# Moving the first batches' weight products, banks and score work in a fused attention and leaky-ReLU kernel

## The chip, the cores and the metric

The kernel runs on one core of one Trainium2 chip. The metric is the device time of one execution in microseconds (us); lower is better. A core has five engines with queues of their own, each worked off in order: TensorE (PE; its weight loads are listed apart as PEld), VectorE (DVE), ScalarE (ACT), GpSimd (POOL) and SyncE (SP), which here issues transfers only. Matmul results go to PSUM, a memory of eight banks of 128 partitions x 512 fp32 values, from which DVE or ACT copies them to SBUF.

## What is computed

```python
B, H, S, Ns, D = 8, 8, 512, 32, 64          # x: (B,H,S,D), state: (B,H,Ns,D)
scores  = x @ state^T / sqrt(D);  a  = softmax(scores);  xread = a @ state     # S rows
scores2 = state @ x^T / sqrt(D);  a2 = softmax(scores2); sread = a2 @ x        # Ns rows
rows = concat([xread, sread], axis=2) -> (B*(S+Ns), H*D) = (4352, 512)
h = rows @ w_in                 # w_in: 512 x 2048
out = max(0.01*h, h) @ w_out    # w_out: 2048 x 512, fp32 result
```

## The kernel before, in words

Products are done in bf16 with fp32 sums. For each batch b the kernel does not form xread. It multiplies the state by w_in first: M = state @ w_in, block by block, 2 x 128 rows by 2048 columns, made in four **quarters** of 512 columns (`a_m`, line 356; copied from PSUM to SBUF by `m_evict`, line 376). Then the hidden layer of the batch is aT (the softmax weights, transposed) times M: sixteen column blocks j of 128, each two matmuls of 512 columns (`ff1`, line 386; for batch 0 `ff1_0`, line 927, two blocks at a time), each followed by the leaky ReLU on ACT (`Prelu`). The second product with w_out runs as `piece` (line 590: four matmuls of 512 columns for rows i and a quarter jq of the 16 blocks) for batch 0 and half of batch 1, and as Strassen-Winograd products of 256 columns for the rest. A **unit** (`Fast.unit`, line 657) is one step of those, two matmuls for batches 2 to 7; `Batch.run(n)` runs n of them. `Half` is the same for the second half of batch 1.

A matmul of a_m or a_scores uses 64 rows and 32 columns of the PE array; eight of these run side by side and are listed as 64*32. The spreads of the head use 128*32, all large products 128*128.

The order of the instructions on every engine is that of the program text (`manual_schedule`, line 52); only the waits come from the framework. PSUM is handed out by tags: "ph" and "py" are two banks each, used in turn, "sc" and "big" are a pair of neighbouring banks each. A new tile in a tag waits until the reader of the old one is done.

**Head** (lines 772 to 1017). Batch 0 has a special softmax in two halves u. For each half PE transposes x (`x0_half`), makes the scores twice (`scores0`, `rows0`), DVE finds the maximum (`max0`) and splits it in a high and a low bf16 part (`split0`: hi, lo), PE subtracts it from the scores by 32 small matmuls (`spread0`, line 816), ACT takes the exponential (`exp0`), PE sums it (`sum0`), DVE takes the reciprocal (`recip0`), PE spreads that (`recip0_rows`) and DVE multiplies (`probs0`, line 864, gives aT). Between the two spreads stand two matmuls on zeros (`spin(2, "py")`, line 900). Then come batch 0's products ff1_0, with the remaining quarters of M and batch 1's quarter 0 between them, batch 0's second scores (`a_scores`, `a_max2`), batch 1's casts, transposes, scores and quarters 1 to 3, with `piece` products between.

The head's loads are issued by POOL in the order w_in chunks 0 to 3 (one chunk holds the columns of one quarter), w_out chunk 0, batch 1's x in two halves, w_out chunks 1 and 2, batch 2's x, w_out chunk 3.

**Batches 2 to 7** (lines 1059 to 1192). Step s of sixteen runs ff1 block s of batch b, some units of the batch before or of the batch itself, as many as the list PACE (PACE2 for b = 2) says, and parts of the next batch's softmax. At s = 10 the first three quarters of the next batch's M are made, in "big", "sc" and "ph". In the last batch the blocks 4 to 11 are made by `FastLast` (line 500: 14 small products `pl`, whose partial sums DVE and ACT copy to tiles `ls`), two to a step; at s = 8 `a_sread` (line 311) makes the batch's sread: 16 matmuls into `psr`, in tag "big", copied by two ACT instructions into sr_t (line 322). At s = 13 `x_sums` reads sr_t, and after the loop `FastIn` multiplies it.

Of the kernel before, what the change touches and what calls it, by code (L numbers as in the profile page):

```python
# [9 lines left out]
P = 128  # L10
B, H, S, D = 8, 8, 512, 64
NS = 32
DFF = 2048
DM = 512
# [5 lines left out]
BF16 = mybir.dt.bfloat16  # L20
FP32 = mybir.dt.float32
# [6 lines left out]
def kernel(  # L28
# [15 lines left out]
    mpool = ctx.enter_context(tc.tile_pool(name="mpool", bufs=2))  # L44
# [84 lines left out]
    def spin(n, tag):  # L129
        p = psum.tile([P, S], FP32, name="pspin", tag=tag, bufs=2 if tag in ("ph", "py") else 1)  # L130
        for _ in range(n):
            nc.tensor.matmul(p[:], lhsT=idle[:, :P], rhs=idle[:], start=True, stop=True)  # L132

    stbd = consts.tile([P, NK, 2, NS], BF16, name="stbd")
    st1 = consts.tile([P, P], BF16, name="st1")
    groups = ((2, 4), (4, 8))
# [40 lines left out]


    class Attn:
        pass

    def a_open(a, b):
        a.b = b
# [165 lines left out]

    def a_m(a, c, tag):
        if c == 0:
            a.M = mpool.tile([P, 2, DFF], BF16, name="M", tag="M")
        if tag in ("ph", "py", "phpy"):
            pm = [psum.tile([P, DM], FP32, name="pm", tag=t) for t in (tag[:2], tag[-2:])]  # L360
            at = [t[:] for t in pm]
        else:
            pm = psum.tile([P, 2, DM], FP32, name="pm", tag=tag, bufs=1)
            at = [pm[:, g, :] for g in range(2)]
        for k in range(NK):
            for g in range(2):
                v, r = (k // 2, 2 * (k % 2) + (g ^ (k // 2))) if a.b == 0 else (g, k)
                nc.tensor.matmul(  # L368
                    at[v][NS * r:NS * (r + 1)],
                    lhsT=st_of(a, g, k),  # L370
                    rhs=w_in_bf[D * g:D * (g + 1), k, DM * c:DM * (c + 1)],
                    start=True, stop=True,
                )
        return pm
# [388 lines left out]

    OWN = 15
    PACE = (1, 4, 4, 4, 3, 4, 4, 3, 4, 4, 4, 4, 3, 4, 3, 3)
    PACE2 = (0,) * 10 + (3, 3, 2, 2, 2, 3)

    att_of = [Attn() for _ in range(B)]
    a0, a1, a2 = att_of[:3]
# [127 lines left out]
    rows0(1)  # L897
    spread0(scn[0], m[0], False)
    exp0(0)
    spin(2, "py")  # L900
    spread0(scn[1], split0(m[1]), False)
    exp0(1)
    sum0(0)
    q = [recip0(0)]
    pm = a_m(a0, 0, "sc")
    for g in range(2):
        SCA(a0.M[:, g, :DM], pm[:, g, :])
    sum0(1)
    q.append(recip0(1))
    for u in range(2):  # L910
        recip0_rows(u, q[u])
        probs0(u)
    m_evict(a0, 1, a_m(a0, 1, "big"), VEC)

    h0 = hpool.tile([P, 16, S], BF16, name="hT", tag="hT")

    def open_ff1_0(tag):  # L920
        if tag == "sc":
            pr = psum.tile([P, 2, S], FP32, name="php", tag=tag, bufs=1)
            return pr, [pr[:, 0], pr[:, 1]]
        ph = [psum.tile([P, S], FP32, name="ph", tag=tag) for _ in range(2)]
        return ph, [p[:] for p in ph]
# [22 lines left out]
    relu0(t0, 0)  # L948
    relu0(t2, 2)
    m_evict(a0, 2, a_m(a0, 2, "big"), VEC)  # L950
    m_evict(a1, 0, a_m(a1, 0, "ph"), VEC)
    for j, tag in ((4, "py"), (6, "sc"), (8, "py"), (10, "ph"), (12, "py"), (14, "ph")):
        t, bk = open_ff1_0(tag)
        for g in range(2):
            ff1_0(bk, j, g)
        relu0(t, j)
        if j == 8:
            m_evict(a0, 3, a_m(a0, 3, "big"), VEC)
            a_scores(a0)
            a_max2(a0)  # L960
    nc.vector.memset(stf[0][:, 0, D - 1:D + 1], 0.0)
# [6 lines left out]

    for g in range(2):
        a_exp2(a0, g)  # L970
    for i in (0, 1):
        piece(0, h0, i, 0)
    wide = psum.tile([P, 2, DM], FP32, name="pyw", tag="big", bufs=1)
    for u in range(2):
        ps = psum.tile([P, NT, 2, P], BF16, name="pxt2", tag="ph")
        for t in range(NT):
            for v in range(2):
                h = NK * u + 2 * v
                nc.tensor.transpose(
                    ps[:, t, v, :], a1.xb[:, t, h:h + 2, :].rearrange("p h d -> p (h d)"), ident[:]  # L980
                )
        VEC(a1.xT[:, :, 2 * u:2 * u + 2, :], ps[:])
        piece(0, h0, 2 + u, 0, bank=wide[:, u])
    a_scores(a1)
    m_evict(a1, 1, a_m(a1, 1, "ph"), SCA)
    a_shift(a1)
    a_max2(a1)
    for i in (0, 1):
# [71 lines left out]
    for b in range(2, B):  # L1060
# [20 lines left out]
        for s in range(16):  # L1081
            fast = nxt is None and 4 <= s < 12
            if fast:
                n = 1 if s in (7, 11) else 2
                k = PACE[s]
                for i in range(n):
                    fl.product()
                    units((i + 1) * k // n - i * k // n)
            elif s == 11:
                fill(s)  # L1090
            if not fast:
                ff1(a, hT, 4 + s if nxt is None and s < 4 else s)
            if s == 0:
                if b + 2 < B:
                    load_x(b + 2, nc.sync)
                a_a2t(a)
                if before:
                    for n in (0, 1):
                        before.f.sums(n, 4, 8)
            elif s == 1:  # L1100
                if nxt is not None:
                    a_scores(nxt)
                m_evict(a, 3, a_m(a, 3, "big"), SCA)
                if b == 2:
                    a_sread_rows([a0])
                elif b % 2:
                    a_sread_rows([att_of[b - 2], att_of[b - 1]])
                if b == 2:
                    half.f.sums(2)
                    a_shift(nxt, 0)  # L1110
                elif nxt is not None:
                    a_shift(nxt)
                if b + 2 < B:
                    open_xb(b + 2)
                    for h in range(0, H, 2):
                        cast_x(b + 2, h, h + 2, POO)
                if before:
                    before.f.sums(2, 4, 8)
            elif s == 3:
                if before:  # L1120
                    before.f.sums(3)
                if nxt is not None and b > 2:
                    a_max2(nxt)
            elif s == 4:
                if b == 2:
                    state_t(1)
                elif b == 4:
                    sread_t(0, 3)
                elif b == 7:
                    sread_t(1, 4)  # L1130
            elif s == 8:
                if nxt is None:
                    a_sread(a)
            elif s == 12:
                for n in range(3):
                    now.f.sums(n, 0, 4)
            if nxt is None:
                if s == 1:
                    fl = FastLast(a, hT)
                    fl.sums()  # L1140
                elif s in (6, 10):
                    fi.w_sum({6: 1, 10: 3}[s])
                elif s == 13:
                    fl.flush()
                    fi.x_sums()
            elif b >= B - 3 and s == 14:
                if b == B - 3:
                    fi = FastIn(None)
                fi.w_sum(2 * (b - (B - 3)))
            if s == (9 if b == 2 else 7) and b + 2 < B:  # L1150
                a_open(att_of[b + 2], b + 2)
                a_xt_dma(att_of[b + 2])
            if nxt is not None:
                if b == 2 and s < 11:
                    if s in (8, 9):
                        a_exp2(nxt, s - 8)
                elif s == 5:
                    a_exp(nxt)
                elif s in (7, 8):
                    a_exp2(nxt, s - 7)  # L1160
                    if s == 7:
                        a_probs(nxt)
                elif s == 11:
                    a_probs2(nxt)
                elif s in (12, 13):
                    SCA(nxt.M[:, s - 12, DM:2 * DM], pm1[:, s - 12, :])
            if std:
                i, jq = std.pop(0)
                piece(1, h1, i, jq)
            elif b == 2 and half.units:  # L1170
                half.run(7)
                if s == 4:
                    a_shift(nxt, 1)
                    half.f.sums(3)
                    weights_sum(3)
                    a_max2(nxt)
                elif s == 6:
                    a_exp(nxt)
                elif s == 8:
                    a_probs(nxt, 0)  # L1180
            elif s != 11 and not fast:
                fill(s)
            if s == 10 and nxt is not None:
                pm0 = a_m(nxt, 0, "big")
                pm1 = a_m(nxt, 1, "sc")
                pm2 = a_m(nxt, 2, "ph")
                for g, copy in enumerate((VEC, SCA)):
                    copy(nxt.M[:, g, 2 * DM:3 * DM], pm2[g][:])
                m_evict(nxt, 0, pm0, SCA)
                if b == 2:  # L1190
                    a_probs(nxt, 1)
# [91 lines left out]
```

## Time and profile before

| What | Value |
|---|---|
| median of 3 runs | 203.49 us (203.1 to 204.0) |
| the profiled execution | 203.36 us |
| its span, first to last instruction | 201.6 us |
| PE busy | 195.9 us, 2000 matmuls |
| DVE, ACT, POOL busy | 159.5, 145.0, 42.6 us |
| granted TensorE clock | 1.0 |
| head: first product of batch 0 | 13.56 us |
| head: first piece (py) | 22.20 us |
| w_in chunks landed | 9.00, 11.54, 15.36, 17.48 us |
| w_out chunks landed | 20.08, 25.27, 28.20, 33.75 us |
| batch 1's x, two halves landed | 21.61, 22.90 us |

The table's lower part is read from the trace, in us from the start of the span. In the lines of a timeline further down, the first number is the start, the second the time from the start of the first to the end of the last instruction of the group, then the engine, the line of the kernel, the operation, output<-inputs, rows*columns of the array, the shape and how many. In the lines of waits, the numbers are the total in us, how often, and the longest. An instruction's duration contains its latency, so durations of neighbours on one engine overlap; what an instruction costs its engine is the step to the next start.

### The profile page before, as it was taken

What the parts mean: (1) busy time and instruction counts of PE and PEld (TensorE: products, weight loads), DVE (VectorE), ACT (ScalarE), POOL (GpSimd) and SP (SyncE); (2) the same over time, 40 slices, a digit from 0 to 9 for tenths busy, and PEclk for the clock granted to TensorE, in tenths of its full rate; (3) what the DMA queues carried; (4) which work ended last, traced back from release to release, by engine and by line L of the source; (5) the groups of instructions that cost most, each with busy time, mean ns of one, the idle gap of its engine ahead of it and who ended that gap; (6) DMA issues with size and microseconds to landing.
All of it is one profiled execution on the core that took longest, in us unless ns stands there. A gap on an engine that the chain in (4) does not pass through costs nothing.

```text
span 201.6 us, 4848 instructions
## 1 busy us (share of the span) xinstructions
PE 195.9 (97%) x2000; PEld 129.2 (64%) x2000; DVE 159.5 (79%) x241; ACT 145.0 (72%) x267; POOL 42.6 (21%) x69
## 2 busy tenths in 40 slices
PE   7899999999999999999999999999999999999993
PEld 2543444444377567766776677676767688799882
DVE  1676679899989889985997599779978977995612
ACT  3459839589869886978697868787878768767710
POOL 8931002021009005200410040200020014104250
PEclk9999999999999999999999999999999999999999
DMA  6999995999794995549343945250029101310035
GB/s 198 218 206 277 232 301 99 133 311 238 131 210 127 123 282 96 104 167 274 81 78 124 281 75 99 107 156 5 0 86 173 31 3 66 142 55 3 0 90 170
DMA packets 39733, 27.99 MB, mean 139 GB/s; under 512 B 25312, under 2 KB 36704, under 8 KB 39712
## 3 DMA queue, kind: packets, MB, share of 16 engines
q1 hardware_dynamic: 34512, 20.88, 43.3%
q0 software_dynamic: 4912, 6.55, 15.9%
q10 hardware_dynamic: 288, 0.26, 0.6%
q8 instruction: 15, 0.25, 0.5%
q14 instruction: 6, 0.05, 0.1%
HBM read 17.30 MB, written 8.91 MB: 130 GB/s over the span
## 4 chain that ended last, share of the span: by engine, by line
PE 96%; DVE 1%; ACT 1%; issue 0%
PE yq L666 40%; PE ph L389 22%; PE py L596 7%; PE pm L368 4%; PE pyw L596 3%; PE pf L463 3%; PE yu L666 3%; PE pspin L132 3%; PE ph L929 2%; PE pl L552 2%; PE sc L207 1%; PE psn L333 1%; PE phw L400 1%; PE php L929 1%; DVE M L382 1%; ACT xT L791 1%
## 5 line engine op out<-in xcount | busy, mean ns | idle before, releaser
L394 ACT ACTIVATE hT<-ph 128x512 bf16<-128x512 f32 x100 | 58.9, 605 | 18.0 <-PE ph L389 17.6
L389 PE MATMUL ph<-aT,M 128*128 128x512 bf16 x200 | 57.8, 379 | 0.0
L666 PEld LDWEIGHTS <-su 128*128 128x128 bf16 x448 | 42.9, 98 | 13.8 <-DVE su L655 0.8
L666 PEld LDWEIGHTS <-hT 128*128 128x128 bf16 x312 | 30.1, 98 | 13.5 <-issue 2.0
L666 PE MATMUL yq<-tw_xf,su 128*128 128x256 bf16 x208 | 29.6, 273 | 0.0
L666 PE MATMUL yq<-w_out_bf,hT 128*128 128x256 bf16 x208 | 29.2, 273 | 0.0
L105 POOL CAST xb<-xl 128x512 bf16<-128x512 f32 (+1 forms) x21 | 14.1, 709 | 59.0 <-DMA xl<-in_x_dram 44.6
L389 PEld LDWEIGHTS <-M 128*128 128x128 bf16 x200 | 19.4, 98 | 7.3 <-issue 0.8
L655 DVE TENSOR_TENSOR su<-hT 128x1024 bf16<-128x1024 bf16 x26 | 18.1, 698 | 7.1 <-ACT hT L394 7.1
L675 ACT COPY sv<-yq 128x512 f32<-128x512 f32 (+1 forms) x28 | 15.4, 555 | 2.1 <-PE yq L666 1.4
L736 POOL TENSOR_TENSOR yo<-sv,sv 128x512 f32<-128x512 f32 x6 | 7.8, 1302 | 40.3 <-ACT sv L675 23.3
L596 PE MATMUL py<-w_out_bf,hT 128*128 128x512 bf16 x64 | 16.0, 379 | 0.0
L596 PEld LDWEIGHTS <-hT 128*128 128x128 bf16 x96 | 9.0, 98 | 10.8 <-issue 0.9
L666 PE MATMUL yq<-tw_x,su 128*128 128x256 bf16 x104 | 14.6, 273 | 0.0
L666 PE MATMUL yq<-w_out_bf,su 128*128 128x256 bf16 x104 | 14.5, 272 | 0.0
L382 ACT CAST M<-pm 128x1024 bf16<-128x1024 f32 x13 | 13.2, 1014 | 0.9 <-PE pm L368 0.9
L666 PE MATMUL yq<-tw_x,hT 128*128 128x256 bf16 x96 | 13.6, 273 | 0.0
L678 DVE TENSOR_TENSOR yo<-yq,sv 128x512 f32<-128x512 f32 x17 | 11.6, 684 | 1.5 <-PE yq L666 1.5
L287 ACT ACTIVATE e<-sc,mcols 128x512 bf16<-128x512 f32 x16 | 11.1, 697 | 0.2 <-DVE mcols L281 0.2
L279 DVE TENSOR_REDUCE mcol<-sc 128x2 f32<-128x1024 f32 x8 | 9.7, 1214 | 0.0
L655 DVE TENSOR_TENSOR su<-su,hT 128x1024 bf16<-128x1024 bf16 x13 | 9.0, 692 | 0.4
L217 DVE TRANSPOSE_TENSOR_REDUCE mrow<-sc 128x32 f32<-128x1024 f32 x7 | 8.7, 1244 | 0.6 <-PE sc L207 0.5
(167 smaller groups left out, 295.7 us busy)
## 6 DMA issues: line engine op xcount, KB each, us to landing
xl<-in_x_dram SPq DMA_DIRECT2D x5, 1024.0 KB, 6.6
out_dram<-yo SPq DMA_DIRECT2D x10, 512.0 KB, 2.7
w_in_bf<-in_moe_w_in_dram POOLq DMA_DIRECT2D x4, 512.0 KB, 9.2
w_out_bf<-in_moe_w_out_dram POOLq DMA_DIRECT2D x4, 512.0 KB, 17.0
out_dram<-ysb SPq DMA_DIRECT2D x8, 256.0 KB, 6.6
xf<-in_x_dram SPq DMA_DIRECT2D x2, 512.0 KB, 4.8
x<-in_x_dram POOLq DMA_DIRECT2D x2, 512.0 KB, 14.0
xl<-in_x_dram POOLq DMA_DIRECT2D x1, 1024.0 KB, 19.4
```

The costliest lines, as they stand in the source:

```text
L105: copy(xs[b][:, :, h0:h1].rearrange("p t h d -> p h t d"), xl[b][:, h0:h1].rearrange("p h (t d) -> p h t d", t=NT),)
L217: nc.vector.tensor_reduce(out=m1[:], in_=flat.rearrange("p (c j) -> p c j", j=NS), axis=AX.X, op=ALU.max, apply_transpose=True,)
L279: nc.vector.tensor_reduce(out=m2[:], in_=a.sc[:], axis=AX.X, op=ALU.max, negate=True)
L287: nc.scalar.activation(out=a.e2[:, g], in_=a.sc[:, g, :], func=AF.Exp, bias=a.m2s[:, g:g + 1], scale=SCALE, accum_out=a.r2[:, g:g + 1],)
L382: copy(a.M[:, :, cols], pm[:])
L389: nc.tensor.matmul(ph[:], lhsT=a.M[:, g, P * j:P * (j + 1)], rhs=a.aT[:, g, :], start=(g == 0), stop=(g == 1),)
L394: nc.scalar.activation(out=hT[:, j, :], in_=ph[:], func=AF.Prelu, alpha=0.01)
L596: nc.tensor.matmul(y.py, lhsT=hT[:, j, P * i:P * (i + 1)], rhs=w_out_bf[:, j, :], start=(j == 0), stop=(j == 15),)
L655: (eng or nc.vector).tensor_tensor(out=S[n][:, ms], in0=u[:, ms], in1=v[:, ms], op=op)
L666: nc.tensor.matmul(bank[:, i, :], lhsT=lhs[:, m, P * i:P * (i + 1)], rhs=rhs[:, m, :], start=(first and m == 0 and (i == 0 or of is not No ...
L675: copy(t[:], bank)
L678: nc.vector.tensor_tensor(out=dst, in0=bank, in1=self.sv[n][:], op=ALU.add)
```

## The change

- `a_m` makes the tile M where there is none yet, so that a quarter may be made out of order.
- The two spins go. In their place stands quarter 0 of batch 1's M (in "py"); DVE copies its first half right behind the second half's lo part, ACT copies its second half behind the two copies of batch 0's quarter 0.
- Quarter 1 of batch 0's M is made right behind quarter 0, and not after the softmax; its copy stays where it was.
- The tags "py", "sc", "py", "sc", "py", "ph", "py", "ph" for the eight double blocks of batch 0 become "py", "sc", "ph", "sc", "py", "ph", "py", "big".
- The copy of batch 0's last quarter is split in two halves of 256 columns. Batch 0's second scores and their maximum come after block pair 10 and not after 8.
- Of batch 1's transposes, each half comes after one piece; scores and quarter 1 come before the last piece of the first four and not after it.
- PACE2 gives 1, 4, 3, 3, 2, 2 units at s = 10 to 15, where it gave 3, 3, 2, 2, 2, 3.
- `a_sread` of the last batch moves from s = 8 to s = 11.

```diff
     class Attn:
-        pass
+        M = None
...
     def a_m(a, c, tag):
-        if c == 0:
+        if a.M is None:
             a.M = mpool.tile([P, 2, DFF], BF16, name="M", tag="M")
...
-    PACE2 = (0,) * 10 + (3, 3, 2, 2, 2, 3)
+    PACE2 = (0,) * 10 + (1, 4, 3, 3, 2, 2)
...
     exp0(0)
-    spin(2, "py")
+    a0.M = mpool.tile([P, 2, DFF], BF16, name="M", tag="M")
+    pm1 = a_m(a1, 0, "py")
     spread0(scn[1], split0(m[1]), False)
+    VEC(a1.M[:, 0, :DM], pm1[0][:])
     exp0(1)
     sum0(0)
     q = [recip0(0)]
-    pm = a_m(a0, 0, "sc")
+    pm = [a_m(a0, 0, "sc"), a_m(a0, 1, "big")]
     for g in range(2):
-        SCA(a0.M[:, g, :DM], pm[:, g, :])
+        SCA(a0.M[:, g, :DM], pm[0][:, g, :])
+    SCA(a1.M[:, 1, :DM], pm1[1][:])
     sum0(1)
...
-    m_evict(a0, 1, a_m(a0, 1, "big"), VEC)
+    m_evict(a0, 1, pm[1], VEC)
...
-        if tag == "sc":
+        if tag in ("sc", "big"):
...
     m_evict(a0, 2, a_m(a0, 2, "big"), VEC)
-    m_evict(a1, 0, a_m(a1, 0, "ph"), VEC)
-    for j, tag in ((4, "py"), (6, "sc"), (8, "py"), (10, "ph"), (12, "py"), (14, "ph")):
+    for j, tag in ((4, "ph"), (6, "sc"), (8, "py"), (10, "ph"), (12, "py"), (14, "big")):
         t, bk = open_ff1_0(tag)
         for g in range(2):
             ff1_0(bk, j, g)
         relu0(t, j)
         if j == 8:
-            m_evict(a0, 3, a_m(a0, 3, "big"), VEC)
+            m3 = a_m(a0, 3, "big")
+            for c in range(0, DM, 2 * P):
+                VEC(a0.M[:, :, 3 * DM + c:3 * DM + c + 2 * P], m3[:, :, c:c + 2 * P])
+        elif j == 10:
             a_scores(a0)
             a_max2(a0)
...
-    for i in (0, 1):
-        piece(0, h0, i, 0)
-    wide = psum.tile([P, 2, DM], FP32, name="pyw", tag="big", bufs=1)
     for u in range(2):
+        piece(0, h0, u, 0)
         ps = psum.tile([P, NT, 2, P], BF16, name="pxt2", tag="ph")
...
         VEC(a1.xT[:, :, 2 * u:2 * u + 2, :], ps[:])
-        piece(0, h0, 2 + u, 0, bank=wide[:, u])
+    wide = psum.tile([P, 2, DM], FP32, name="pyw", tag="big", bufs=1)
+    piece(0, h0, 2, 0, bank=wide[:, 0])
     a_scores(a1)
     m_evict(a1, 1, a_m(a1, 1, "ph"), SCA)
+    piece(0, h0, 3, 0, bank=wide[:, 1])
     a_shift(a1)
...
-            elif s == 8:
-                if nxt is None:
-                    a_sread(a)
...
                 elif s in (6, 10):
                     fi.w_sum({6: 1, 10: 3}[s])
+                elif s == 11:
+                    a_sread(a)
```

## The prediction

> **What bounds the kernel now.** I read the page's busy shares and its chain first, then TensorE's (PE's) timeline at the three places that the change touches, the waits of its weight loads (PEld) there, and the timelines of ScalarE (ACT) and VectorE (DVE) beside them.
>
> ```profile
> PE 195.9 (97%) x2000; PEld 129.2 (64%) x2000; DVE 159.5 (79%) x241; ACT 145.0 (72%) x267; POOL 42.6 (21%) x69
> PE 96%; DVE 1%; ACT 1%; issue 0%
> ```
>
> PE is busy for 195.9 of 201.6 us and is 96% of the chain, so a change gains only what it takes out of PE's own queue where PE waits for nothing else. In a timeline the step from one start to the next tells the cost: a 512-wide matmul takes 0.216 in a run (eight of py in 1.73). In the head:
>
> ```profile
> 10.21 0.60 PE L132 MATMUL pspin<-idle 128*128 128x512 bf16 x2
> 10.74 0.24 PE L820 MATMUL scn<-ident,hi 128*32 128x128 bf16 x4
> ...
> 13.22 0.41 PE L368 MATMUL pm<-w_in_bf,stbd 64*32 64x512 bf16 x8
> 13.56 0.61 PE L929 MATMUL ph<-aT,M 128*128 128x512 bf16 x2
> ...
> 15.40 0.41 PE L368 MATMUL pm<-w_in_bf,stbd 64*32 64x512 bf16 x8
> 15.63 0.40 PE L368 MATMUL pm<-w_in_bf,st 64*32 64x512 bf16 x8
> 15.96 1.04 PE L929 MATMUL ph<-aT,M 128*128 128x512 bf16 x4
> ...
> 18.69 0.41 PE L368 MATMUL pm<-w_in_bf,stbd 64*32 64x512 bf16 x8
> 18.97 0.41 PE L207 MATMUL sc<-xT,stbd 64*32 64x512 bf16 x8
> 19.32 3.04 PE L929 MATMUL ph<-aT,M 128*128 128x512 bf16 x12
> 22.20 1.89 PE L596 MATMUL py<-w_out_bf,hT 128*128 128x512 bf16 x8
> ```
> ```profile
> PEld L929 <- DVE M L382: 0.6, 1, 0.6
> PEld L368 <- DMA w_in_bf<-in_moe_w_in_dram: 0.4, 1, 0.4
> PEld L820 <- DVE lo L836: 0.4, 1, 0.4
> ```
>
> See three waits: the second half's spread (10.74) waits for VectorE's lo part; the quarter at 15.40 waits for the third chunk of w_in; and twelve matmuls from 19.32 take 2.88 where 2.59 would do, because M's last quarter is not copied yet.
>
> **Head, before 15.40: worth nothing.** The two spins stand in a wait: lo runs on DVE 10.49 to 10.67, and the spread starts 0.07 later with or without them. Batch 1's quarter 0 goes there: eight 64x32-tile matmuls, 0.22, plus the price of changing tile shape. That price is in the rows: four pyw from 25.68 to 26.64 take 0.96 where the four from 24.37 take 0.86 (0.10 to go in), and the pm at 26.86 takes 0.33 where the sc before it takes 0.22 (0.11 to come out). So it runs from about 10.10 to 10.53, with 0.14 of cover; without cover it costs up to 0.43. Its chunk landed at 9.00 by the trace. Its copies fit: DVE's 0.68 behind lo, before the 11.59 where DVE idled 0.93; ACT's 0.59 at 13.0, where ACT idled 1.59 until 14.63. Quarter 1 of batch 0 moves from 13.22 to behind quarter 0 (11.49): 16 matmuls in one visit end at about 12.01, and the instruction behind waits for the exponential (ACT 11.42 plus 0.60) until 12.07 anyway; its chunk landed at 11.54. What this frees at 13.22 is taken back at once: the first product needs the first aT (DVE, two in 1.30 from 12.79, the first done near 13.45), so 0.06 is gained, and the quarter at 15.40 still needs the chunk that landed at 15.36. Zero, taken from that row.
>
> **Head, 15.40 to 22.20: -0.35.** (a) The quarter at 15.63 is gone: a visit of two takes 0.56, of one 0.34 (13.22): -0.22. (b) VectorE loses batch 1's two copies (0.68 each) and copies M's last quarter in two halves. With the quarter's matmuls now at about 18.48, the halves are done near 19.6 and 20.25, and the products that read them start at 20.1 and 21.0: the 0.29 goes, and 0.04 at 17.70 with it. (c) Quarter and scores, one visit before (0.62 from 18.69 to 19.32), become two with a product between: 0.33 each and 0.10 to go in once more, +0.14. (d) PE then runs close to ACT: the product on sc waits for its bank until relu(t2), ACT 15.61 plus 1.03, so 16.68 instead of 16.61: +0.07. Laid out on one line: 15.40, 15.74, 16.68, 17.54, quarter 18.48, product 18.81, scores 19.78, products 20.11 and 20.98, end 21.84 against 22.20; (a) to (d) give -0.34. Other banks are free in time: py since 15.6, ph at 17.6, big when its last half is copied (20.25, needed 20.98).
>
> The Trainium skill's page "TensorEngine Tiling (Array Packing)", section Tiling Modes, says that changing the tiling mode drains the engine. It speaks against (c), gives no figure, and the 0.10 and 0.11 above agree; without the split, (c) would be zero and the head -0.5.
>
> **21.84 to 65: nothing.** Pieces, transposes and scores are the same instructions in another order (transposes next to pieces show no price: 0.45 for eight at 23.92 and 25.23). The second transposes, now at 24.0, need batch 1's second half, cast on DVE by 23.62 after landing at 22.90; cover 0.3 where there was 1.6. The scores, at 25.41, need xT, done at about 25.35 on DVE. The later w_out chunks landed at 25.27, 28.20 and 33.75, needed at 26.8, 31.2 and 34.6. SP's and POOL's queues keep their order; xT of batch 2 landed at 39.43, needed at 39.9. So -0.35 is carried on.
>
> **PACE2: +0.1.** Before, three units (six 256-wide matmuls, 0.65) stand on each side of batch 3's three quarters of M, and two waits for a ph bank cost 0.14 (67.12 to 67.92 for six) and 0.12 (ahead of the product at 69.34).
>
> ```profile
> 66.34 0.84 PE L368 MATMUL pm<-w_in_bf,st_t 64*32 64x512 bf16 x24
> 67.12 0.83 PE L666 MATMUL yq<-w_out_bf,hT 128*128 128x256 bf16 x6
> 67.92 1.02 PE L389 MATMUL ph<-aT,M 128*128 128x512 bf16 x4
> ...
> 66.06 0.61 ACT L394 ACTIVATE hT<-ph 128x512 bf16<-128x512 f32 x1
> ```
>
> The last row is ACT's. After, four matmuls fewer stand ahead, so the quarters start 0.44 earlier, at 65.91 on this clock; but the third needs the ph bank which ACT frees at 66.67, a row that moves only with ACT's own queue. It starts at 66.72 instead of 66.78, the product after the eight matmuls at 67.93 instead of 67.92 with one unit (0.22) still owed, and the second wait (0.12) is gone: +0.1. If ACT kept ahead, both waits would go: -0.26. Both ends are kept; I take +0.1, by the ACT row.
>
> **Rows read later: +0.36.** Here what is moved was itself the filling of a wait:
>
> ```profile
> 167.23 0.60 PE L666 MATMUL yq<-w_out_bf,su 128*128 128x256 bf16 x4
> 167.67 0.63 PE L315 MATMUL psr<-a2T,xb 128*128 128x64 bf16 x16
> 168.14 0.38 PE L552 MATMUL pl<-lx,lw 128*128 128x256 bf16 x2
> ...
> 167.38 0.60 ACT L565 COPY ls<-pl 128x512 f32<-128x512 f32 x1
> 168.40 0.53 ACT L322 CAST sr_t<-psr 64x128 bf16<-64x128 f32 x2
> ```
>
> The product at 168.14 overwrites the bank that ACT copies until 167.98. Without psr's 0.47 it starts at 168.03, not 167.67. The next (168.79) waits for DVE's join (168.02 plus 0.69) and keeps 168.77. Later two waits shrink, because ACT has no sr_t copies (0.53) ahead of the next ls: 0.14 at 169.58, of which DVE's copy for the product at 170.34 leaves 0.11. At the new place, after 171.97, PE has no wait that psr could fill: the next product starts without one at 172.08, and the timeline to the end is back to back. So 0.47 is added and 0.11 gained: +0.36. Bounds: +0.47 with nothing gained, +0.2 if the two waits (0.14 and 0.10) and a little more go.
>
> **Sum.** -0.35 + 0.1 + 0.36 = +0.1 on the profiled execution's 203.36 (span 201.6 and 1.8 around it): 203.5. The median shown, 203.49, is 0.13 above that execution, and its runs span 203.1 to 204.0.
>
> **Rivals.**
> - *Every wait that the change names is worth its length.* Spins 0.53, quarters 0.34 and 0.22, M's copy 0.33, PACE2 0.26, the ACT waits 0.24 come to 1.9: 201.5. For it: all of these are in the timeline. Against: lo at 10.67 and the w_in chunk at 15.36 stand behind the first two. The Trainium skill, "Perfetto Trace Analysis", section Matmul Optimizations, says that all 8 PSUM banks should be in use, which is what the four pairs do. 0.09, with what lies between it and the forecast.
> - *The tail's moves do work and the head too:* -0.35 - 0.26 + 0.2, or 202.95. 0.2; still within 0.5%.
> - *Slower: the moved-up transposes meet batch 1's second half.* If it lands later than 23.2, PE, in order, stands still behind them, with pieces, scores and all else queued behind. The two halves landed 1.29 apart; one such spacing late is about 1.0 beyond the cover: 204.5. Against: no transfer before 22.9 is moved. 0.1.
> - *It doesn't do what it says:* products on four pairs don't run ahead because ACT (8 pairs at about 1.03 each, 14.6 to 22.9) paces them; the head then keeps -0.1: 203.7. 0.13.
>
> The forecast has 0.48. 0.5%, about 1.0 us, is what a measurement of this kernel can tell from no change. Faster by more: 0.09; slower by more: 0.11; within: 0.80. The range takes in the unknowns (-0.26 to +0.1, +0.2 to +0.47, -0.5 to 0 in the head), the runs' scatter of 0.5 and the late half: 202.5 to 204.5.
>
> **What would show it.** Right: the spread still starts at 10.7, the quarter still at 15.4 behind its DMA; the first py at 21.8; no wait for M in between; the third quarter of batch 3 behind ACT; psr's 0.47 uncovered near 172 and the pl product near 168.03 behind the ACT copy. Wrong: a spread or an exponential sum later than now (a landing late, DVE's new copy in the way); transposes waiting on xb; a first py at 22.2 or later; product after psr's old place at 167.7.

## The result, and the profile after

The changed kernel takes 203.86 us (median of 22 runs, 203.24 to 204.46) against 203.39 (22 runs, 202.85 to 204.0): the ratio is 1.0023, with a 95% interval of 1.0013 to 1.0032, so 0.3 to 0.65 us slower. The forecast was +0.1, within 0.5%, range 202.5 to 204.5. That it is slower, and by less than 0.5%, came out as forecast. The size did not: +0.47 on the medians against +0.1, and the interval leaves +0.1 out. One term that was put at nothing costs 0.3 on average.

The profiled execution took 203.91 us, its span is 202.1. The first two lines are the page's busy shares and its chain.

```profile
PE 194.5 (96%) x1975; PEld 129.1 (64%) x1998; DVE 159.2 (79%) x241; ACT 145.6 (72%) x267; POOL 42.7 (21%) x69
PE 88%; DVE 5%; ACT 2%; DMA 2%; issue 1%; DVEq 0%
```

PE still sets the end. It lists 25 matmuls fewer though the program has lost only the two spins: some records are missing in this trace, so a group may say x3 where four ran. Steps between starts of groups are not touched by that. Here is PE's timeline of the head after the change.

```profile
10.30 0.41 PE L366 MATMUL pm<-w_in_bf,st 64*32 64x512 bf16 x8
10.79 0.24 PE L818 MATMUL scn<-ident,hi 128*32 128x128 bf16 x4
...
11.51 0.25 PE L844 MATMUL r<-ones,e 128*128 128x4 bf16 x4
11.70 0.74 PE L366 MATMUL pm<-w_in_bf,stbd 64*32 64x512 bf16 x16
12.37 0.25 PE L844 MATMUL r<-ones,e 128*128 128x4 bf16 x4
...
15.65 0.41 PE L366 MATMUL pm<-w_in_bf,stbd 64*32 64x512 bf16 x8
15.99 1.04 PE L929 MATMUL ph<-aT,M 128*128 128x512 bf16 x4
16.94 1.02 PE L929 MATMUL php<-aT,M 128*128 128x512 bf16 x4
17.80 1.03 PE L929 MATMUL ph<-aT,M 128*128 128x512 bf16 x4
18.76 0.41 PE L366 MATMUL pm<-w_in_bf,stbd 64*32 64x512 bf16 x8
...
21.29 1.03 PE L929 MATMUL php<-aT,M 128*128 128x512 bf16 x3
22.15 1.03 PE L594 MATMUL py<-w_out_bf,hT 128*128 128x512 bf16 x4
```

From the third quarter to the first py it now takes 22.15 - 15.65 = 6.50, before 6.79 (15.40 to 22.20, rounded): the wait for M is gone, as forecast. But this execution came to the third quarter 0.25 later. Part of that is not the kernel's: its first loads landed 0.5 later. Part is: the sixteen pm from 11.70 take 0.67 to the next start, where a visit of two quarters needs 0.56 (15.40 to 15.96 before), because w_in's chunk 1 landed at 11.99.

To keep such scatter apart from the change, PE's timeline of every run is cut at the same groups. **sum** is from the first exponential sum (`r<-ones`) to batch 0's first product, **quarter** from the third quarter of batch 0's M to the first py, **pieces** from there to batch 1's first product, **pace** from the first yq to batch 4's scores, **rows** from the last psn (products of the state rows of earlier batches) to the first pf (`FastIn`). Start is the time of that first sum. The stages not shown agree but for two: from batch 4's scores to the last psn it is 84.30 in every run, and from the first pf to the end 24.94 to 24.97; from the first product to the third quarter it is 1.82 to 1.84, but 1.88 in e8 and 2.03 in e3; from batch 1's first product to the first yq it is 19.2 or 19.3.

| run | start | sum | quarter | pieces | pace | rows |
|---|---|---|---|---|---|---|
| before | 11.30 | 2.26 | 6.79 | 14.53 | 17.30 | 19.02 |
| changed | 11.51 | 2.32 | 6.50 | 14.53 | 17.63 | 19.38 |
| e1_rows_back | 10.85 | 2.75 | 6.50 | 14.53 | 17.83 | 19.01 |
| e2_pace_back | 10.86 | 2.83 | 6.50 | 14.68 | 17.43 | 19.38 |
| e3_head_only | 11.15 | 2.26 | 6.42 | 14.54 | 17.30 | 19.01 |
| e4_rows_only | 10.71 | 2.26 | 6.79 | 14.82 | 17.30 | 19.38 |
| e5_quarter1_only | 11.66 | 2.57 | 6.79 | 14.53 | 17.30 | 19.01 |
| e6_head_quarter1_back | 11.45 | 2.26 | 6.50 | 14.66 | 17.44 | 19.01 |
| e7_no_spin | 11.31 | 2.26 | 6.79 | 14.54 | 17.30 | 19.02 |
| e8_quarter1_back_pace3 | 11.25 | 2.26 | 6.46 | 14.53 | 17.26 | 19.01 |
| e9_pace_only | 11.54 | 2.26 | 6.79 | 14.53 | 17.43 | 19.01 |
| e10_quarter1_chunk0 | 11.49 | 2.23 | 6.79 | 14.53 | 17.43 | 19.01 |
| e11_scores_beside | 11.51 | 2.26 | 6.37 | 14.64 | 17.43 | 19.01 |
| e12_beside_pace4 | 12.14 | 2.26 | 6.37 | 14.53 | 17.16 | 19.01 |

The start differs by 1.4 us over the runs, more than any stage does: by 0.95 between the five profiles that still have the spins, whose code is the same up to there, and by 1.3 between the eight with batch 1's quarter 0 in their place. That is why whole times of single runs say little here.

### The profile page after: what moved, and what is told of

The parts are those of the page before. It is cut to its first block, busy times and chain, and to the rows that moved or that the text cites. A ratio compares the mean times of both kernels' runs of the same rounds, so it can differ in the third digit from the quotient of the medians.

```text
span 202.1 us, 4822 instructions
## 1 busy us (share of the span) xinstructions
PE 194.5 (96%) x1975; PEld 129.1 (64%) x1998; DVE 159.2 (79%) x241; ACT 145.6 (72%) x267; POOL 42.7 (21%) x69
## 3 DMA queue, kind: packets, MB, share of 16 engines
HBM read 17.30 MB, written 8.91 MB: 130 GB/s over the span
## 4 chain that ended last, share of the span: by engine, by line
PE 88%; DVE 5%; ACT 2%; DMA 2%; issue 1%; DVEq 0%
PE yq L664 37%; PE ph L387 19%; PE py L594 7%; PE pm L366 4%; PE pyw L594 3%; PE pf L461 3%; PE yu L664 3%; PE ph L929 2%; DMA st0f<-in_state_dram 2%; PE pl L550 2%; PE sc L206 1%; PE php L929 1%; PE psn L332 1%; DVE tw_x L630 1%; PE phw L398 1%
## 5 line engine op out<-in xcount | busy, mean ns | idle before, releaser
L387 PE MATMUL ph<-aT,M 128*128 128x512 bf16 x183 | 54.9, 379 | 0.3
L105 POOL CAST xb<-xl 128x512 bf16<-128x512 f32 (+1 forms) x21 | 13.0, 658 | 56.3 <-DMA xl<-in_x_dram 45.0
L387 PEld LDWEIGHTS <-M 128*128 128x128 bf16 x200 | 19.3, 98 | 6.9 <-issue 0.6
## 6 DMA issues: line engine op xcount, KB each, us to landing
xl<-in_x_dram POOLq DMA_DIRECT2D x1, 1024.0 KB, 19.3
```

The source lines that it names most:

```text
L105: copy(xs[b][:, :, h0:h1].rearrange("p t h d -> p h t d"), xl[b][:, h0:h1].rearrange("p h (t d) -> p h t d", t=NT),)
L387: nc.tensor.matmul(ph[:], lhsT=a.M[:, g, P * j:P * (j + 1)], rhs=a.aT[:, g, :], start=(g == 0), stop=(g == 1),)
```

## The experiments

Theory A, formed from the two traces: the rows' move costs 0.36, PACE2 about 0.3, the head gains a little. The rivals were that the head itself is slower and the tail neutral (B), that PACE2 gains (C), and, once the stages were seen, rivals for the pieces of the head (D to H). All ratios are to the kernel before, run on the same chip; they are not those of the two medians and can differ a little from them.

### Taking the parts back, one at a time

e1_rows_back:
```diff
+            elif s == 8:
+                if nxt is None:
+                    a_sread(a)
...
-                elif s == 11:
-                    a_sread(a)
```

> The changed kernel with the last batch's a_sread back at s = 8; all else as changed. Theory A (the rows' 0.47 is uncovered near 172 and filled a wait near 167.7; PACE2 waits for ACT; the head gains a little): 0.36 less than the changed kernel, so about +0.1 on the kernel before (203.5); in the profile psr starts near 167.9 and no wait stands ahead of the pl product behind it. Theory B (the head itself is slower, since its first product came 0.27 later in the changed profile; the tail's edits are neutral): as the changed kernel, 203.9.

Measured: 203.45 against 203.27, ratio 1.0000 (0.9986 to 1.0014). The rows stage is 19.01, as before, and psr starts at 167.83, as A has it; B's 203.9 lies outside the interval. This run also showed what A had not counted, in the head:

```profile
11.04 0.41 PE L366 MATMUL pm<-w_in_bf,stbd 64*32 64x512 bf16 x8
11.80 0.41 PE L366 MATMUL pm<-w_in_bf,stbd 64*32 64x512 bf16 x8 [0.36 <-DMA w_in_bf<-in_moe_w_in_dram]
12.15 0.25 PE L844 MATMUL r<-ones,e 128*128 128x4 bf16 x4
```

These are quarter 0, quarter 1 and the second exponential sum. The second eight stand in the sixteen's place but PE waits for chunk 1, which landed at 11.76; the sum behind them, whose exponential was done at 11.57, is held too, and the softmax with it (2.75 where 2.26 was).

e2_pace_back:
```diff
-    PACE2 = (0,) * 10 + (1, 4, 3, 3, 2, 2)
+    PACE2 = (0,) * 10 + (3, 3, 2, 2, 2, 3)
```

> The changed kernel with PACE2 as before (3, 3, 2, 2, 2, 3). Theory A: 0.3 less than the changed kernel, about +0.15 on the kernel before; the 24 pm matmuls of batch 3's quarters take 0.77 and not 1.35. Theory B: as the changed kernel, 203.9. Theory C (PACE2 does what the earlier start of the quarters suggests and gains 0.26; the head costs what is left): 0.26 more than the changed kernel, 204.1.

Measured: 203.55 against 203.27, ratio 1.0011 (0.9999 to 1.0022). The pace stage is 17.43 where the changed kernel has 17.63, so C falls; the rows stage keeps its 19.38. A's 0.77 for the 24 pm is missed: they take 0.91 here, with the old counts, and the stage is not back at 17.30. What the other 0.13 is stands under the pace of batch 2.

e3_head_only is both of these edits.

> Only the head of the change: a_sread and PACE2 as before. Theory A: 0.2 (0.05 to 0.35) faster than the kernel before, about 203.2, and the first py near 21.9 to 22.1. Theory B: 0.4 slower than before, 203.8.

Measured: 203.28 against 203.27; the ratio 1.0020 has an interval of 0.9993 to 1.0047, since two of its twelve runs lie above 205, with a granted clock of 0.988 where the other ten have 0.997 to 1.0. The median shows neither B's +0.4 nor A's -0.2, and the interval is too wide to settle it. The profiled execution is 201.2 long and follows the line laid out in the prediction:

```profile
15.44 0.41 PE L366 MATMUL pm<-w_in_bf,stbd 64*32 64x512 bf16 x8
15.78 1.04 PE L929 MATMUL ph<-aT,M 128*128 128x512 bf16 x4
16.66 1.03 PE L929 MATMUL php<-aT,M 128*128 128x512 bf16 x4
17.52 1.03 PE L929 MATMUL ph<-aT,M 128*128 128x512 bf16 x4
18.48 0.41 PE L366 MATMUL pm<-w_in_bf,stbd 64*32 64x512 bf16 x8
...
19.78 0.41 PE L206 MATMUL sc<-xT,stbd 64*32 64x512 bf16 x8
...
21.86 1.03 PE L594 MATMUL py<-w_out_bf,hT 128*128 128x512 bf16 x4
```

So the gain of 0.3 behind the third quarter is real. Something ahead of it, seen in e1 and e2 (2.75, 2.83) but not here (2.26), can take it back in a part of the executions.

e4_rows_only is the kernel before with a_sread at s = 11.

> The kernel before with a_sread at s = 11 as the only edit. Theory A: +0.36, about 203.75; the pl product behind the old place starts some 0.36 behind the end of the units ahead of it, behind ACT's copy, and psr's 0.47 stands near 172 with no wait ahead of it. Theory B: as before, 203.4.

Measured: 203.64 against 203.27, ratio 1.0015 (1.0003 to 1.0027); the rows stage is 19.38 against 19.02. PE's timeline of this run:

```profile
166.81 0.60 PE L666 MATMUL yq<-w_out_bf,su 128*128 128x256 bf16 x4
167.61 0.38 PE L552 MATMUL pl<-lx,lw 128*128 128x256 bf16 x2 [0.20 <-ACT ls L565]
...
171.12 0.60 PE L666 MATMUL yq<-w_out_bf,hT 128*128 128x256 bf16 x4
171.55 0.63 PE L315 MATMUL psr<-a2T,xb 128*128 128x64 bf16 x16
172.02 0.38 PE L389 MATMUL ph<-aT,M 128*128 128x512 bf16 x1
```

The four yq need 0.44 and take 0.80: without psr, PE waits 0.36 for ACT's copy of the bank. At the new place the units ahead of psr take their 0.43 and psr its 0.47: nothing is waited for there. The same two steps, 0.80 and 0.47, stand in the changed kernel's trace and in e2's. A holds, B falls. The steps in between go as forecast too: counted from the last psn, the pl behind the old place starts 0.11 earlier than before, the next one 0.03, the one after that 0.17, and the fifth again 0.11, which is what is left at the end against psr's 0.47.

### The head's own terms

e5_quarter1_only moves quarter 1 of batch 0 in the kernel before, and nothing else:
```diff
-    pm = a_m(a0, 0, "sc")
+    pm = [a_m(a0, 0, "sc"), a_m(a0, 1, "big")]
     for g in range(2):
-        SCA(a0.M[:, g, :DM], pm[:, g, :])
+        SCA(a0.M[:, g, :DM], pm[0][:, g, :])
...
-    m_evict(a0, 1, a_m(a0, 1, "big"), VEC)
+    m_evict(a0, 1, pm[1], VEC)
```

> The kernel before with one edit: batch 0's quarter 1 behind quarter 0, ahead of the second exponential sum. Theory A (in the executions where x lands early, the quarter now waits for w_in's chunk 1, and the softmax waits behind it): slower by 0.3 (0 to 0.5), about 203.6; its second eight matmuls start within 0.1 of the chunk's landing where that is later than 11.5, and from the first exponential sum to the first product it takes more than the 2.26 of before, up to 2.8. Theory D (the cover of 0.06 and the equal landings hold; the head's small gain has another cause): 203.3, no difference.

Measured: 203.64 against 203.47, ratio 1.0020 (1.0006 to 1.0034); the sum stage is 2.57. Chunk 1 landed at 12.38 and the second eight start at 12.42, by this run's timeline:

```profile
11.66 0.25 PE L846 MATMUL r<-ones,e 128*128 128x4 bf16 x4
11.84 0.41 PE L368 MATMUL pm<-w_in_bf,stbd 64*32 64x512 bf16 x8
12.42 0.41 PE L368 MATMUL pm<-w_in_bf,stbd 64*32 64x512 bf16 x8 [0.17 <-DMA w_in_bf<-in_moe_w_in_dram]
12.76 0.25 PE L846 MATMUL r<-ones,e 128*128 128x4 bf16 x4
```

e10_quarter1_chunk0 takes the cause away and keeps the order: quarter 1 is computed from chunk 0's columns (cw is 0 for quarter 1 of batch 0, and c otherwise), so that quarter of M holds other numbers.
```diff
-                    rhs=w_in_bf[D * g:D * (g + 1), k, DM * c:DM * (c + 1)],
+                    rhs=w_in_bf[D * g:D * (g + 1), k, DM * cw:DM * (cw + 1)],
```

> As the kernel before with quarter 1 moved behind quarter 0, but the matmuls of quarter 1 read w_in's chunk 0, which is there by then, so that nothing waits for chunk 1; it computes batch 0's hidden blocks 4 to 7 from wrong columns. Theory A (the DMA wait is what the move of quarter 1 costs): 2.26 from the first exponential sum to the first product, or 0.06 less, and the time of the kernel before, 203.4. Theory G (the sixteen matmuls in a row are what delays the second sum): as quarter 1 moved alone, 0.2 to 0.4 slower than before.

Measured: 203.33 against 203.45, ratio 0.9993 (0.9983 to 1.0002). Chunk 1 landed at 12.66 here, later than in any run above, and nothing waits for it:

```profile
11.49 0.25 PE L847 MATMUL r<-ones,e 128*128 128x4 bf16 x4
11.67 0.63 PE L369 MATMUL pm<-w_in_bf,stbd 64*32 64x512 bf16 x16
12.26 0.25 PE L847 MATMUL r<-ones,e 128*128 128x4 bf16 x4
```

The sum stage is 2.23. A holds and G falls: the cost of moving quarter 1 is the transfer, not the sixteen matmuls. In the five profiles that have the move and read chunk 1 (changed, e1, e2, e3, e5) the cost, which is the sum stage less 2.26, equals the chunk's landing less the start, less 0.42, to 0.01: the chunk landed 0.48, 0.91, 0.99, 0.42 and 0.72 behind the start. In the nine others it landed 0.24 to 1.16 behind it. With the same 0.42 the move would have cost 0.3 on average over all fourteen profiles, as an estimate; the 0.24 is that of the kernel before, the smallest of all.

e6_head_quarter1_back is e3 with quarter 1 back at its old place.

> The head of the change without the move of batch 0's quarter 1; a_sread and PACE2 as before. Theory A: the gain from the third quarter's place to the first py (0.3) is kept and nothing is lost ahead of it: 0.3 faster than before, about 203.0; 2.26 from the first exponential sum to the first product. Theory D: as the head alone, 203.3.

Measured: 203.27 against 203.47, ratio 0.9994 (0.9982 to 1.0006); sum 2.26, quarter 6.50. The head's stages are A's, but the medians are 0.20 apart, the ratio says 0.12, and its interval holds both 0.3 and nothing. In this execution the second half of batch 1's x landed at 23.55, and the moved-up transposes waited for its cast (waits of weight loads in 23 to 25 us):

```profile
PEld L979 <- DVE xb L966: 0.4, 1, 0.4
```

The piece ahead of them takes 0.98 where 0.86 is enough (23.35 to 24.33): 0.12 of the 0.3 is lost, and pieces shows 14.66. The pace stage, with the old PACE2, is 17.44 and not 17.30, which takes as much again.

e7_no_spin is the kernel before without `spin(2, "py")`.

> The kernel before without the two spins, nothing in their place. Theory A (they stand in the wait for lo): no difference, 203.3, the second spread still starts 0.06 behind lo's end. Rival E (what stands in PE's queue counts in full): 0.5 faster, 202.8. Rival F (the idle stretch lowers the granted clock): slower by 1 or more, with matmuls of twice the step behind 10.2.

Measured: 203.39 against 203.47, ratio 1.0002 (0.9990 to 1.0014); the sum stage is that of before. PE stands idle, and the spread starts when DVE is ready:

```profile
9.96 0.23 PE L820 MATMUL scn<-ident,lo 128*32 128x128 bf16 x4
10.60 0.24 PE L820 MATMUL scn<-ident,hi 128*32 128x128 bf16 x4 [0.41 <-DVE hi L833]
10.81 0.24 PE L820 MATMUL scn<-ident,lo 128*32 128x128 bf16 x4
```

DVE's hi is done at 10.54 and its lo at 10.75, so each group of four starts 0.06 behind the part that it reads; the first does not wait for lo. The granted clock stays at 1.0 and a group of the spread still steps by 0.06, so E and F fall. In the kernel before it is otherwise: hi was done at 10.45 and lo at 10.66, but the spread starts at 10.74, behind the spins of 10.21, and its first lo group comes no sooner than this:

```profile
10.81 0.23 PE L820 MATMUL scn<-ident,lo 128*32 128x128 bf16 x4
```

From the end of lo to the first sum it takes 0.64 there, 0.64 in e4 and 0.66 in e5, and 0.56 in all the others. So the spins did cost up to 0.1 in three of the five profiles that have them, too little for the medians to tell.

e11_scores_beside is e6 with a_scores and a_max2 right behind the last quarter:
```diff
             for c in range(0, DM, 2 * P):
                 VEC(a0.M[:, :, 3 * DM + c:3 * DM + c + 2 * P], m3[:, :, c:c + 2 * P])
-        elif j == 10:
             a_scores(a0)
             a_max2(a0)
```

> The head without the move of quarter 1, and batch 0's second scores again right behind its last quarter, so that both are one visit of the 64x32 tiles. Theory A: 0.14 off the stretch from the third quarter to the first py (6.36 and not 6.50), unless the scores wait for the sc bank (ACT frees it near 18.75, they come at 18.70); 0.4 faster than before, about 203.0. Rival H: the changes of tile shape cost nothing that the scores' wait for sc doesn't give back: as the head without the move of quarter 1.

Measured: 203.29 against 203.45, ratio 0.9989 (0.9977 to 1.0000); the quarter stage is 6.37 instead of 6.50.

```profile
18.71 0.41 PE L366 MATMUL pm<-w_in_bf,stbd 64*32 64x512 bf16 x8
19.03 0.41 PE L206 MATMUL sc<-xT,stbd 64*32 64x512 bf16 x8
19.37 1.90 PE L929 MATMUL ph<-aT,M 128*128 128x512 bf16 x8
```

Both together take 0.66; in the changed kernel the two visits take 0.34 each and one more way in. The 0.13 is the price of the extra change of tile shape, some 0.22 for going in and coming out, less 0.10 that the scores wait (0.32 to their start, where 0.22 is enough). H falls by the stage; the times alone would not decide it. That a change of tiling mode drains the engine, as the Trainium skill's page "TensorEngine Tiling (Array Packing)", section Tiling Modes, has it, agrees with these steps.

### The pace of batch 2

e9_pace_only is the kernel before with the new PACE2.

> The kernel before with the new PACE2 (1, 4, 3, 3, 2, 2) as the only edit. Theory A (the third of batch 3's quarters waits for a ph bank that ACT frees behind its exponentials, whenever PE comes): slower by 0.35 (0.1 to 0.5), about 203.7; the 24 pm matmuls take 1.2 or more and not 0.77, and their last group starts within 0.1 of the end of ACT's leaky ReLU. Theory C (the two waits behind the quarters go, nothing takes their place): 0.26 faster, 203.1.

Measured: 203.44 against 203.45, ratio 1.0005 (0.9996 to 1.0013); the pace stage is 17.43. In PE's timeline the quarters wait as A says, in ACT's the leaky ReLU that frees the bank ends at 66.81:

```profile
66.04 1.22 PE L368 MATMUL pm<-w_in_bf,st_t 64*32 64x512 bf16 x24
67.19 1.05 PE L666 MATMUL yq<-w_out_bf,hT 128*128 128x256 bf16 x8
```
```profile
66.20 0.61 ACT L394 ACTIVATE hT<-ph 128x512 bf16<-128x512 f32 x1
```

The mechanism is A's (1.15 for the 24 pm and not 0.77); the stage is 0.13 longer and not 0.35, and C's gain of 0.26 is not there. The new counts bring PE to the quarters 0.43 earlier (9.88 behind the first yq and not 10.31), and ACT does not follow. In the changed kernel the same 24 take 1.35, by PE's and ACT's timelines:

```profile
65.77 1.42 PE L366 MATMUL pm<-w_in_bf,st_t 64*32 64x512 bf16 x24
67.12 1.05 PE L664 MATMUL yq<-w_out_bf,hT 128*128 128x256 bf16 x8
```
```profile
64.31 0.69 ACT L286 ACTIVATE e<-sc,mcols 128x512 bf16<-128x512 f32 x1 [0.37 <-DVE mcols L280]
...
66.13 0.60 ACT L392 ACTIVATE hT<-ph 128x512 bf16<-128x512 f32 x1
```

The exponentials ahead of the leaky ReLU wait 0.37 for DVE's mcols here, and 0.17 in the kernel before and in e9. This wait is not the change's: it is also 0.37 in e10, whose only edit is in quarter 1, which has the old PACE2 and comes to this stage no earlier than the kernel before (first yq at 56.06 and 56.03); its stage is 17.43 as well and not 17.30. Here are DVE's and POOL's rows ahead of mcols, two of before, then DVE, POOL and ACT in e10:

```profile
60.37 0.68 DVE L655 TENSOR_TENSOR su<-hT,su 128x1024 bf16<-128x1024 bf16 x1
60.76 3.43 POOL L105 CAST xb<-xl 128x512 bf16<-128x512 f32 x4 [14.43 <-ACT sv L675]
...
60.40 0.93 DVE L656 TENSOR_TENSOR su<-hT,su 128x1024 bf16<-128x1024 bf16 x1
58.50 2.29 POOL L105 CAST xb<-xl 128x512 bf16<-128x512 f32 x4 [13.50 <-DMA xl<-in_x_dram]
64.48 0.69 ACT L287 ACTIVATE e<-sc,mcols 128x512 bf16<-128x512 f32 x1 [0.37 <-DVE mcols L281]
```

VectorE makes su and tw_x for the Strassen-Winograd products; POOL casts a later batch's x and state. In all fourteen profiles this su takes 0.68 when no cast of POOL is running at its start (before, e3, e5, e7, e8, e9, e12) and 0.92 to 1.12 when one is (the seven others). The tw_x behind it takes 1.21 or 1.22 in e4 and e12 and 1.62 or 1.63 elsewhere, and the casts are longer as well where the two meet. So DVE and POOL hold each other up here, and whether they meet goes with when that x has landed. This is read from the traces; no run moved POOL's casts alone.

With the old counts the stage is 17.30 where the wait for mcols is 0.17 or less, and 17.43 where it is 0.37 (e2, e6, e10, e11). With the new counts it is 17.43 at 0.17 (e9), 17.63 at 0.37 (the changed kernel) and 17.83 at 0.57 (e1). At the same wait PACE2 thus costs 0.13 and 0.20; the other 0.13 of the changed profile's 0.33 would have been there without it.

e8_quarter1_back_pace3 and e12_beside_pace4 try other counts, e8 the first of these on e6, e12 the second on e11:
```diff
-    PACE2 = (0,) * 10 + (3, 3, 2, 2, 2, 3)
+    PACE2 = (0,) * 10 + (3, 4, 3, 2, 2, 1)
+    PACE2 = (0,) * 10 + (3, 4, 2, 2, 2, 2)
```

> As the head without the move of quarter 1, and PACE2 as 3, 4, 3, 2, 2, 1: the units ahead of batch 3's quarters stay three, more stand behind them. Theory A: the quarters start as late as before and so don't wait for ACT (0.77 for 24 pm), and the two waits of 0.14 and 0.12 behind them are filled: 0.55 faster than before, about 202.75. Rival: the waits are ACT's and DVE's and only move on: 203.0.

> As the run with the scores beside the quarter, and PACE2 as 3, 4, 2, 2, 2, 2. Theory A: eight matmuls behind the quarters fill the first wait (0.14) and half of the second (0.12), and two units at the last step leave time for the leaky ReLU that they read: another 0.2 off, 202.8. Rival: waits move on, as with 3, 4, 3, 2, 2, 1, and it is worth less than 0.1.

Measured, e8: 203.25 against 203.47, ratio 0.9987 (0.9970 to 1.0005), pace 17.26. Both waits behind the quarters are gone, but the single unit of the last step and the one after it now wait 0.1 each for hidden blocks that ACT has not finished: the rival is right. e12: 203.17 against 203.45, ratio 0.9990 (0.9977 to 1.0002), pace 17.16, so 0.14 is kept of the 0.26, more than the rival's 0.1 and less than A's 0.2. e12's median lies below both kernels'. Its interval against the kernel before still holds 1, so it is not shown to be faster than that; it ends below the changed kernel's interval (1.0013 to 1.0032), so it is faster than that one, each measured against the kernel before.

## Why the prediction was right, and where it was short

- **Spins worth nothing:** right within what the times can tell (e7, ratio 1.0002, 0.9990 to 1.0014). The reading under it was not: in the very profile that was read the spread started behind the spins and not behind lo, and taking them out is worth up to 0.1 in such an execution, which works for the change.
- **Quarter 1 behind quarter 0 worth nothing:** this step failed. The prediction put 0.06 of cover there, "its chunk landed at 11.54", from one execution. What the runs showed is a race between two loads: the softmax starts when x is there (first sum at 10.7 to 12.1), chunk 1 lands on its own time (11.5 to 13.0). When the quarter stood at 13.22, the race didn't matter. Moved, it costs 0.06, 0.49, 0.57, 0 and 0.31 in the five profiles that have it (sum stage less 2.26), on average near 0.3; e10 shows that the transfer is the cause. The profile that was read had the most room of all fourteen. The list of what would make the prediction wrong named a late landing, the sum gave it nothing.
- **The third quarter's chunk as the floor (15.36):** it held PE back in e3 (0.20) and a little in e8 (0.05). In the profile that was read, chunk and PE came together by chance: the step from the first product to the third quarter is 1.84 there, and 1.82 to 1.84 wherever the chunk landed clearly earlier (in e7 at 15.26, with the quarter at 15.40 all the same). So the quarter did not wait for the chunk, as the prediction read it, and in most runs a delay of the softmax was passed on in full.
- **15.40 to 22.20, -0.35:** right in mechanism and nearly in size: -0.29 in four of the six runs with this order, -0.33 in e8 and -0.37 in e3, the two whose third quarter waited for its chunk.
- **21.84 to 65, nothing:** right in five of the eight profiles with this order; in e2, e6 and e11 the transposes waited 0.11 to 0.15 for batch 1's second half (landed at 23.47 to 23.55), the rival's mechanism at about a tenth of its price. It isn't the change's alone: e4, with the old order, waited 0.29 when that half landed at 23.71.
- **PACE2, +0.1:** right in mechanism, a little too small: the third quarter does wait for the bank that ACT frees, and that costs 0.13 where ACT is as early as in the profile that was read, 0.20 where ACT is 0.2 later. That ACT's time hangs on DVE and POOL, with the old counts too, had no term.
- **Rows, +0.36:** right, to 0.01, in every run that has the move, and step by step.
- **Sum:** by the changed profile's stages, +0.06 - 0.29 + 0.33 + 0.36, less 0.10 between batch 1's first product and the first yq (19.20 for 19.30, a step that scatters between these two values with the old code too), is +0.36, and 0.2 of a later start makes the span's +0.55. On the median it is +0.47 (0.26 to 0.65). As an estimate over executions, quarter 1's 0.3, the head's -0.29, the rows' 0.36 and PACE2's 0.13 to 0.20, less up to 0.1 for the spins, come to +0.4 to +0.57. What the forecast lacked is thus mainly quarter 1's wait. That the time still lies within 0.5% is owed to the width of that band, not to this term.

What stays open: the head alone came out at +0.0 in the median, which fits a gain of 0.3 against quarter 1's 0.3 on average, but its interval is too wide to show it, and why two of its runs lie above 205 isn't known. What POOL's casts cost the pace stage was not tested by moving them.

## What to carry to other kernels

A matmul moved up in an in-order queue takes its own inputs' waits with it, and everything behind it then waits too; before costing such a move at nothing, read the spread of the two landings over several executions, not the order in one. An instruction group that stands in a wait is nearly free there (0.11 of psr's 0.47): moving it away uncovers both the wait and the group. A gain made early is kept only as far as the next wait for something that did not move with it (in e3 the third quarter waited 0.20 for its chunk). And before a longer stage is laid to an edit, see whether runs without the edit show it as well: 0.13 of the pace stage's 0.33 did.

## What the runs showed of the hardware

The first loads' landings differ by 0.9 us from execution to execution (batch 0's first half of x at 5.08 to 5.78 in most runs, 6.00 in e12), the third w_in chunk's by 1.4 (14.17 to 15.54), with the same instructions ahead of them. A short idle stretch of PE of 0.4 us, in e7, left the granted clock at 1.0. The tensor-tensor operation su on DVE, over 128x1024 bf16, took 0.68 us on its own and 0.92 to 1.12 when a POOL cast was running at its start.
